# Fused recurrence, MoE and SwiGLU kernel: raw weight loads behind the capacity branch, and a rewritten attention tail

## The chip, the cores and the metric

The kernel runs on one core of one Trainium2 chip. The metric is device microseconds of one launch, inputs and outputs in device memory. Lower is better.

## The reference, cut to what matters

Three layers follow each other. A decayed recurrence over 768 steps (2 batches, 8 heads of width 48) gives 1536 rows of 384 values. A top-1 mixture of 8 experts with a capacity of 384 rows each maps them to 1536 rows, and a SwiGLU layer of inner width 1536 gives the output.

```python
cur = np.einsum('bhd,bhe->bhde', u[None] * kt, vt)
y[:, :, t] = np.einsum('bhd,bhde->bhe', rt, state + cur)
state = wt[:, :, :, None] * state + np.einsum('bhd,bhe->bhde', kt, vt)
...
expert_idx = np.argmax(x @ w_gate, axis=1)       # probs: softmax of the same logits
# rows go to their expert's slots in order, up to capacity
h = np.maximum(np.einsum('ecd,edf->ecf', disp, w1), 0.0)
y = np.einsum('ecf,efd->ecd', h, w2)
out[i] = gate_w[i] * y[expert_idx[i], pos[i]]    # rows that were kept
...
return (silu(x @ w_gate) * (x @ w_val) @ w_out)
```

## The kernel before

**Stages.** The sequence is cut into 12 units of 128 rows (u = 0 to 11, six per batch). A loop does units 0 to 9, and a hand-written piece of straight code, the tail, does the rest of units 10 and 11 and the routing of the last rows. Then comes a branch, then the expert stage (8 experts, at most 240 rows each), then SwiGLU. There is no scheduler: every engine gets its instructions in the order in which the Python code is written, and each waits on semaphores.

**Routing.** Rows are routed in four groups: units 0 to 3, 4 to 7 (`four`), 8 and 9 (`two`), 10 and 11 (`last`). For a group, `chosen_of` gives the steps that find the best expert from the gate products `lg` (`mx`, `eq`, `ls`, `be`, `ohs`, all on DVE, with one `ex` on ACT); `count` numbers the rows per expert on PE; `place` turns this into row addresses `slots`. `rows...` scale the rows into `xg` on ACT, and `scatter` writes them by address to the DRAM buffer `scr`, an indirect DMA on the POOL queue.

**Expert 0.** Its input is not read back whole. The rows of `two` and `last` that belong to it are picked by products with one-hot matrices `hot`: `x0_high` (ACT) and `x0_low` (DVE) split a scaled row block `xhl` into a high and a low half, `x0_add` (L810) adds its product to three PSUM tiles, and the rows scattered earlier come in through `zrow`, read back by `x0_load`. `parts` (L815, L816) then writes the operand `xe0`. The first product of expert 0 reads `xe0`.

**The branch.** `totals` and `offsets` give the counts `cnti`. Every engine loads one of them (L1096) and branches (L1223) around code for overfull experts (label `rare`), which is not taken here. The compiler counts DMA completions and instructions on semaphores, one for each of the eight hardware DMA queues and each engine. On the path that is not taken, each semaphore must be raised by what the skipped code would have added. The instruction for this waits first until everything issued earlier on that semaphore is done. SP does it for the eight DMA queues:

```text
SP L1223 EventSemaphore: wait DMAHW1 >= 144, then add 848
```

ACT's first instruction of expert 0, the ReLU at L1290, waits for all eight raised values, because its tile lies on memory that the skipped code also uses.

**Weights.** Raw float32 weights are loaded in pieces of 768 KB (`raw`, L169) by `load_raws`, as far as buffers are free: four and two from the start, three more (`more_raws(RAWS[2])`) in the tail once the attention buffers are closed by `early.close()`. A raw piece is cut into three parts; each is cast on ACT (`high`, L207) and its remainder computed on DVE (`low`, L212) into one of four, later seven, slots `wu`. These steps stand in a list, and `fill(us)` takes the next ones from it, as much as a credit in microseconds allows (a `low` costs 0.6, a `high` nothing); `need` forces them.

**Expert products.** `m1` (L1284) makes a [128, 240] tile from nine products into one of four PSUM buffers; `relu` (ACT L1290, DVE L1291) frees it; `m2` (L1302) follows after eight such tiles. `warm(n)` (L452) issues n products whose result nobody reads.

## Time and profile before

| | |
|---|---|
| median of 3 runs | 475.51 us (473.94, 475.51, 476.43) |
| profiled execution | 477.18 us, its span 475.5 us |
| PE busy | 452.9 us (95%), 3579 products |
| DVE busy | 332.6 us (70%) |
| ACT busy | 240.3 us (51%) |
| POOL busy | 69.3 us (15%) |
| share of PE in the chain that ended last | 72% |

The span runs from the first to the last instruction; the run's own time has 1.7 us around it. The loop over units lasts until about 78 us, the tail until about 100 us, the experts until about 243 us, and SwiGLU to the end. A product of PE is listed with a modelled end, so products that follow each other overlap in the listing. The granted clock of TensorE is given as a share of full speed, 1.00 or 0.50.

### The profile page before, as it was taken

What the parts mean: (1) busy time and instruction counts of PE and PEld (TensorE: products, weight loads), DVE (VectorE), ACT (ScalarE), POOL (GpSimd) and SP (SyncE); (2) the same over time, 40 slices, a digit from 0 to 9 for tenths busy, and PEclk for the clock granted to TensorE, in tenths of its full rate; (3) what the DMA queues carried; (4) which work ended last, traced back from release to release, by engine and by line L of the source; (5) the groups of instructions that cost most, each with busy time, mean ns of one, the idle gap of its engine ahead of it and who ended that gap; (6) DMA issues with size and microseconds to landing.
All of it is one profiled execution on the core that took longest, in us unless ns stands there. A gap on an engine that the chain in (4) does not pass through costs nothing.

```text
span 475.5 us, 9303 instructions
## 1 busy us (share of the span) xinstructions
PE 452.9 (95%) x3579; PEld 400.9 (84%) x3590; DVE 332.6 (70%) x705; ACT 240.3 (51%) x561; POOL 69.3 (15%) x87
## 2 busy tenths in 40 slices
PE   6998899777999999999999999999999999999994
PEld 3676677667999999999988888888888888888884
DVE  8999999836798658559779966575868576434241
ACT  4566775715788677665455465353525333221220
POOL 3323365430000000000000370000000000003033
PEclk9999999987999999999999999999999999999999
DMA  7899993393989965027323425042200000001011
GB/s 241 191 299 283 323 260 138 108 324 101 287 279 342 307 240 187 12 68 217 116 78 123 71 64 116 17 121 80 66 1 1 2 0 1 0 1 66 0 68 66
DMA packets 33649, 62.57 MB, mean 132 GB/s; under 512 B 5216, under 2 KB 16992, under 8 KB 33600
## 3 DMA queue, kind: packets, MB, share of 16 engines
q1 hardware_dynamic: 31680, 57.20, 40.0%
q0 software_dynamic: 1920, 4.73, 2.7%
q8 instruction: 29, 0.48, 0.4%
q14 instruction: 20, 0.16, 0.1%
HBM read 52.48 MB, written 9.44 MB: 130 GB/s over the span
## 4 chain that ended last, share of the span: by engine, by line
PE 72%; issue 2%; DVE 1%; POOL 1%; POOLq 0%; ACT 0%; ACTq 0%
PE psg L1395 31%; PE psu L1418 14%; PE pso L1302 14%; PE psh L1284 13%; POOL out L1430 1%; PE psx L1269 1%; DVE acc L1428 0%; DVE wu L212 0%; POOLq L1534 0%; DVE h L1291 0%; ACT h L1290 0%; POOLq L1430 0%; ACTq L1290 0%
## 5 line engine op out<-in xcount | busy, mean ns | idle before, releaser
L1395 PE MATMUL psg<-yb,wu 128*128 128x512 f32 x648 | 156.3, 395 | 0.0
L1395 PEld LDWEIGHTS psg<-yb,wu 128*128 128x128 f32 x648 | 121.3, 188 | 26.2
L1418 PE MATMUL psu<-wu,a 128*128 128x384 f32 x432 | 80.8, 336 | 0.0
L1418 PEld LDWEIGHTS psu<-wu,a 128*128 128x128 f32 x432 | 76.4, 188 | 2.9
L1284 PE MATMUL psh<-xe,wu 128*128 128x240 f32 x576 | 72.4, 283 | 6.2 <-DVE h L1291 4.4
L1284 PEld LDWEIGHTS psh<-xe,wu 128*128 128x128 f32 x576 | 68.8, 196 | 7.1 <-DVE h L1291 4.6
L1302 PE MATMUL pso<-h,wu 128*128 128x240 f32 x576 | 66.4, 275 | 0.0
L1302 PEld LDWEIGHTS pso<-h,wu 128*128 128x128 f32 x576 | 65.4, 189 | 0.0
L212 DVE TENSOR_TENSOR wu<-raw,wu 128x512 fp32r<-128x512 f32 x96 | 61.7, 683 | 0.0
L1402 DVE TENSOR_TENSOR t<-t,psg 128x512 f32<-128x512 f32 x36 | 24.7, 686 | 52.6 <-PE psg L1395 35.6
L207 ACT CAST wu<-raw 128x512 fp32r<-128x512 f32 x96 | 55.1, 621 | 3.4 <-PE pso L1302 1.4
L1407 ACT CAST a<-t 128x512 fp32r<-128x512 f32 x36 | 22.3, 619 | 58.2 <-DVE t L1402 58.2
L1291 DVE SCALAR_TENSOR_TENSOR h<-psh,h 128x240 fp32r<-128x240 f32 x64 | 24.9, 402 | 32.3 <-ACT h L1290 32.1
L1317 POOL DMA_INDIRECT idl<-ids,dests x12 | 13.4, 1120 | 171.5 <-DVE bits L187 168.2
L207 ACT CAST wu<-bits 128x384 fp32r<-128x384 f32 x36 | 18.0, 514 | 40.0 <-DVE bits L200 40.0
L1430 POOL DMA_INDIRECT out<-acc,idc x12 | 11.7, 976 | 174.1 <-DVE acc L1428 172.3
L1401 ACT ACTIVATE t<-psg 128x512 f32<-128x512 f32 x36 | 21.4, 595 | 27.5 <-PE psg L1395 27.5
L1290 ACT ACTIVATE h<-psh 128x240 fp32r<-128x240 f32 x64 | 23.3, 374 | 19.3 <-PE psh L1284 10.4
L1408 DVE TENSOR_TENSOR a<-t,a 128x512 fp32r<-128x512 f32 x36 | 24.8, 689 | 11.7 <-ACT a L1407 11.7
L1428 DVE TENSOR_TENSOR acc<-psu,acc 128x384 f32<-128x384 f32 x24 | 12.9, 558 | 20.8 <-PE psu L1418 20.8
L465 ACT COPY A<-psA 128x512 f32<-128x512 f32 x24 | 12.8, 587 | 18.8 <-PE psA L463 18.8
L466 POOL TENSOR_SCALAR_AFFINE_SELECT A<-A 128x512 f32<-128x512 f32 x24 | 15.2, 657 | 44.3 <-ACT A L465 44.3
(154 smaller groups left out, 558.1 us busy)
## 6 DMA issues: line engine op xcount, KB each, us to landing
raw<-in_moe_w SPq DMA_DIRECT2D x32, 768.0 KB, 6.7
dm<-in_dm SPq DMA_DIRECT2D x18, 291.0 KB, 6.7
scr<-zrow SPq DMA_DIRECT2D x12, 384.0 KB, 7.2
raw<-in_moe_w_gate SPq DMA_DIRECT2D x6, 768.0 KB, 4.3
raw<-in_moe_w_val SPq DMA_DIRECT2D x6, 768.0 KB, 4.4
raw<-in_moe_w_out SPq DMA_DIRECT2D x6, 768.0 KB, 4.3
v<-in_tk SPq DMA_DIRECT2D x12, 192.0 KB, 7.8
dm<-in_dm SPq DMA_DIRECT2D x3, 512.0 KB, 5.7
```

The lines of the kernel that those rows point to most:

```text
L207: nc.scalar.copy(out=slot_t[u % NSLOT][:, 0, c:c + n], in_=bits[i])
L212: nc.vector.tensor_tensor(out=w[:, 1, c:c + n], in0=bits.pop(i), in1=R(w[:, 0, c:c + n]), op=ALU.subtract)
L1284: nc.tensor.matmul(ps, w[:, a, k, c0:c0 + 128], xet[e][:, b, k, :], start=n == 0, stop=n == 8)
L1290: nc.scalar.activation(out=h[:, 0, :], in_=ps, func=AF.Relu)
L1291: nc.vector.scalar_tensor_tensor(out=h[:, 1, :], in0=ps, scalar=0.0, in1=R(h[:, 0, :]), op0=ALU.max, op1=ALU.subtract)
L1302: nc.tensor.matmul(ypt[e, d], w[:, a, f % 4, 128 * d:128 * d + 128], h[:, b, :], start=f == 0 and n == 0, stop=f == 7 and n == 2)
L1395: nc.tensor.matmul(gps[i][g], w[:, a, g, k, c0:c0 + 128], yb[t, k][:, c], start=a_ == k == 0, stop=a_ == k == 2)
L1401: nc.scalar.activation(out=t, in_=pg[0], func=AF.Silu)
L1402: nc.vector.tensor_tensor(out=t, in0=t, in1=pg[1], op=ALU.mult)
L1407: nc.scalar.copy(out=a[:, 0], in_=t)
L1408: nc.vector.tensor_tensor(out=a[:, 1], in0=t, in1=R(a[:, 0]), op=ALU.subtract)
L1418: nc.tensor.matmul(out_ps[t, j], att[i][:, c, 128 * j:128 * j + 128], w[:, a, f % 4, :], start=f % FP == 0 and n == 0, stop=f % FP == FP - ...
```

## The change

1. `load_raws` does nothing while `st["held"]` is set. It is set at the start of the tail and cleared behind the branch, after `x_load(1)`; six raw pieces are then issued at once. `early.close()` and `more_raws(RAWS[2])` move behind the tail and behind the branch.
2. The six casts of weight units 0 and 1, formerly three in the loop at u = 5 and three in the tail, stand in the loop at u = 6 and u = 8. The three `low` steps of unit 0 stay in the tail, at other places.
3. In the tail, `values(u + 1, [1, 2, 3])` is one run; `prep3` (DVE tile `rk`) comes after the placing of `four`; `count(two)` comes after `logits(u)`; the scatters of `four` follow their rows one by one; those of `two` move from ahead of the last products to behind them.
4. The low halves of `two` are made on GpSimd from `xg` (`xhl<-xg,xhl`), and their six products move behind those of the high halves of `last`.
5. `warm(2)` goes, and `warm(3)` comes after `count(last)`.

```diff
-            if i > 1:
+            wsteps += [(u, 0.6, low, j) for j in range(4) if i == 6]
...
+            if i > 5:
...
+        if q in xgs:
+            nc.gpsimd.tensor_tensor(out=lo, in0=xgs[q], in1=R(hi), op=ALU.subtract)
+            return
...
-        if u >= 5:
-            fill(0.0)
+        if u in (6, 8):
+            for _ in range(3):
+                step()
...
+    st["held"] = True
...
-    prep3(u + 1)
-    values(u, [2])
-    gate_t(u - 1)
     place(four)
...
     flush()
-    rows4[0]()
+    prep3(u + 1)
+    values(u, [2])
+    gate_t(u - 1)
...
-    values(u + 1, [1, 2])
+    values(u + 1, [1, 2, 3])
+    fill(0.6, 3.0)
...
-    early.close()
-    more_raws(RAWS[2])
-    load_raws(len(raws_))
...
-    x0_add(xhl[two[0]][0], hot[0][:, 0, :], 0, first=True)
-    for i, q in enumerate(two):
-        x0_low(q, sm2[:, i, :])
     for f in rows2:
         f()
+    for i, q in enumerate(two):
+        x0_low(q, sm2[:, i, :])
+    fill(0.6, 3.0)
     judge()
...
-        x0_add(xhl[q][1], hot[0][:, i, :], 0)
+        x0_add(xhl[q][0], hot[0][:, i, :], 0, first=not i)
...
     count(last)
+    warm(3, ps1, "T")
     atl, bases, placed, after = place(last)
-    for f in (*bases, *sums):
+    for f in (*bases, *placed, *sums):
         f()
+    tc.mark_branch_hint_location("rare", engines=[DVE, ACT, POOL])
+    for i, q in enumerate(last):
+        x0_high(q, sm[:, i, :])
+    for i in range(2):
+        onehot(2 + i, *(x[:, i, :] for x in atl))
     flush()
-    for f in later:
-        f()
+    later[0]()
+    totals(ps1, ones, (ohacc, *(ohs[:, q, :] for q in (*two, *last))), odds)
+    offsets(one8)
+    for i, q in enumerate(last):
+        x0_add(xhl[q][0], hot[0][:, 2 + i, :], 0)
+    for i, q in enumerate(two):
+        x0_add(xhl[q][1], hot[0][:, i, :], 0)
...
+    for f in later[1:]:
+        f()
     for q in two:
         scatter(q)
...
     x_load(1)
+    st["held"] = False
+    load_raws(len(raws_))
```

**SP at the branch.** Before, the last rows of SP ahead of the branch: the two reads of `zrow`, four raw pieces, then the load of the count.

```order
L784 DMA zrow<-scr 128x384
L784 DMA zrow<-scr 112x384
L169 DMA raw<-in_moe_w 128x4x384 x2
L169 DMA raw<-in_moe_w 128x3x512 x2
L1096 TENSOR_LOAD cnti
L1223 COMPARE_AND_BRANCH
```

Now, the same place of SP:

```order
L340 DMA v<-in_tk 128x384
L785 DMA zrow<-scr 128x384
L785 DMA zrow<-scr 112x384
L1100 TENSOR_LOAD cnti
L1227 COMPARE_AND_BRANCH
```

And now, SP behind the branch, where the reads of expert 1's rows (`xr`) come first:

```order
L1264 DMA xr<-scr 128x384
L1264 DMA xr<-scr 112x384
L169 DMA raw<-in_moe_w 128x4x384 x2
L169 DMA raw<-in_moe_w 128x3x512 x2
L169 DMA raw<-in_moe_w 128x4x384 x2
L1264 DMA xr<-scr 128x384
```

The four raw pieces went from ahead of the branch to behind it and behind `xr`; two more follow them there.

**DVE, the last choice.** Before, DVE between the best-expert steps of `last` and its one-hot matrices (`within` and `odds` judge the recurrence, `pcs` to `slots` finish the places of `two`):

```order
L580 RECIPROCAL sm<-sm 128x2
L386 TENSOR_SCALAR within<-within 128x1
L389 TENSOR_SCALAR odds<-within 128x1
L680 COPY pcs<-lg 128x16
L700 TENSOR_SCALAR end_1613<-sl 128x2
L703 TENSOR_TENSOR end<-end,sl 128x2
L706 TENSOR_TENSOR slots<-end,end_1613 128x2
L695 TENSOR_TENSOR t_1696<-lg,ohs 128x16
L670 TENSOR_REDUCE sl<-t_1696 128x2
L790 TENSOR_SCALAR hot<-col,end,sl 128x240 x2
```

Now:

```order
L696 TENSOR_TENSOR t_1682<-lg,ohs 128x16
L671 TENSOR_REDUCE sl<-t_1682 128x2
L624 TENSOR_REDUCE sm<-ex 128x2
L578 TENSOR_SCALAR sm<-sm 128x2
L581 RECIPROCAL sm<-sm 128x2
L791 TENSOR_SCALAR hot<-col,end,sl 128x240 x2
L387 TENSOR_SCALAR within<-within 128x1
L390 TENSOR_SCALAR odds<-within 128x1
L681 COPY pcs<-lg 128x16
```

Six small steps that stood ahead of `hot` stand behind it.

**DVE, unit 9 and 10.** Before, `rk`, which PE's gate products of unit 11 read, came straight after the row block `x` of unit 9, ahead of the placing of `four`:

```order
L527 TENSOR_TENSOR x<-y,aV 128x384
L428 TENSOR_TENSOR rk<-dm_112 128x512
L658 TENSOR_SCALAR t_1485<-lg 128x32
L661 TENSOR_TENSOR t_1486<-lg,csb 128x32
L680 COPY pcs<-lg 128x32
L664 TENSOR_TENSOR t_1486<-t_1486,t_1485 128x32
```

Now, the end of the same stretch:

```order
L581 RECIPROCAL sm<-sm 128x4
L671 TENSOR_REDUCE sl<-t_1475 128x4
L674 CAST slots<-sl 128x4
L678 TENSOR_REDUCE ohacc<-ohs 128x8
L429 TENSOR_TENSOR rk<-dm_112 128x512
L528 TENSOR_TENSOR x<-y,aV 128x384
```

`rk` went behind eleven small steps, to the place right ahead of the row block of unit 10.

## Rows read from the trace of the kernel before

**Rows 1.** The chain that ended last, in order of time, at expert 7
```profile
226.84 8.06 PE psh L1284 x72
```
**Rows 2.** Busy time by stretch: PE, PEld, DVE, ACT, POOL; granted clock; DMA share; GB/s
```profile
95.00:100.00 5.00, 4.46 (x24) 4.14 (x23) 3.51 (x15) 2.05 (x5) 3.57 (x4) 0.66 0.95 299
100.00:105.00 5.00, 4.30 (x36) 4.11 (x36) 0.30 (x1) 0.00 (x0) 0.69 (x1) 1.00 1.01 371
110.00:115.00 5.00, 4.35 (x19) 3.79 (x18) 3.58 (x8) 2.64 (x8) 0.00 (x0) 0.50 0.60 177
```
**Rows 3.** Timeline around the branch: start, duration, instruction, idle time and its releaser
```profile
100.61 4.30 PE L1284 MATMUL psh<-xe,wu 128*128 128x240 f32 x36 [1.15 <-ACTq L1223]
108.42 0.37 ACT L1290 ACTIVATE h<-psh 128x240 fp32r<-128x240 f32 x1 [8.56 <-SPq L1223]
...
109.28 1.21 PE L1284 MATMUL psh<-xe,wu 128*128 128x240 f32 x4 [4.37 <-DVE h L1291]
...
117.28 2.18 PE L1302 MATMUL pso<-h,wu 128*128 128x240 f32 x18
```
**Rows 4.** Line L1223, the branch: count, duration in ns, first and last start
```profile
L1223 SPq EVENT_SEMAPHORE  x9: 17/17/17, 97.8 to 108.3; - x9
...
L1223 ACTq EVENT_SEMAPHORE  x2: 17/17/17, 100.5 to 100.6; - x2
```
**Rows 5.** SP in the timeline, then DMA issues of 94 to 101 us (landing time last)
```profile
92.81 2.12 SPq L169 DMA_DIRECT2D raw<-in_moe_w  x4
...
raw<-in_moe_w SPq DMA_DIRECT2D x2, 768.0 KB, 13.9
```
**Rows 6.** The page's costliest groups, two of DVE: count | busy us, mean ns | idle
```profile
L212 DVE TENSOR_TENSOR wu<-raw,wu 128x512 fp32r<-128x512 f32 x96 | 61.7, 683 | 0.0
...
L1291 DVE SCALAR_TENSOR_TENSOR h<-psh,h 128x240 fp32r<-128x240 f32 x64 | 24.9, 402 | 32.3 <-ACT h L1290 32.1
```
**Rows 7.** Landing times: scatters of 84 to 92 us, of 94 to 108, raw pieces to 130
```profile
DMA to landing us min/median/max: 2.6/2.8/3.1
...
DMA to landing us min/median/max: 6.9/7.0/7.7
...
DMA to landing us min/median/max: 4.4/9.2/14.9
```
**Rows 8.** Timeline of ACT, two places in the loop and one at expert 0
```profile
67.55 1.07 ACT L465 COPY A<-psA 128x512 f32<-128x512 f32 x2 [2.06 <-PE psA L463]
...
73.09 0.38 ACT L400 COPY wm<-dm 128x224 f32<-128x224 f32 x1 [1.62 <-DMA dm<-in_dm]
...
122.48 3.22 ACT L207 CAST wu<-raw 128x512 fp32r<-128x512 f32 x6
```
**Rows 9.** Timeline of DVE in the tail
```profile
81.46 1.01 DVE L428 TENSOR_TENSOR rk<-dm 128x512 f32<-128x512 f32 x1
...
91.38 0.17 DVE L606 TENSOR_REDUCE mx<-lg 128x2 f32<-128x16 f32 x1 [0.41 <-PE lg L565]
...
93.20 0.13 DVE L386 TENSOR_SCALAR within<-within 128x1 f32<-128x1 f32 x1
...
94.26 0.72 DVE L790 TENSOR_SCALAR hot<-col,end,sl 128x240 fp32r<-128x240 f32 x2
...
95.05 1.14 DVE L804 SCALAR_TENSOR_TENSOR xhl<-x,sm,xhl 128x384 fp32r<-128x384 f32 x2
```
**Rows 10.** Timeline of PE in the tail
```profile
82.61 0.43 PE L435 MATMUL psr<-rk,ud 128*32 128x128 f32 x8
...
83.18 0.39 PE L488 MATMUL y<-Sb,M 128*64 128x96 f32 x4
...
94.81 2.11 PE L810 MATMUL x<-hot,xhl 128*128 128x240 f32 x10 [0.87 <-DVE hot L790]
```
**Rows 11.** Timeline: a GpSimd product and a small DVE step beside it
```profile
82.93 0.83 POOL L443 TENSOR_TENSOR aV<-v,a 128x384 f32<-128x384 f32 x1
...
83.04 0.77 DVE L667 TENSOR_TENSOR t<-t,ohs 128x32 f32<-128x32 f32 x1
```

More of the change, by code (lines that the diff above doesn't have):

```diff
@@ L128, in build @@
     raw_t, bits, mags, soon = {}, {}, {}, []
-    st = dict(loaded=0, step=0, freed=0, ahead=0.0, made=0)
+    st = dict(loaded=0, step=0, freed=0, ahead=0.0, made=0, held=False)
     def wu(key):
@@ L157, in load_raws @@
     def load_raws(upto):
-        while st["loaded"] < min(upto, len(raws_)):
+        while not st["held"] and st["loaded"] < min(upto, len(raws_)):
             free_ = [p for p in rps if len(p[2]) < p[1] or p[2][-p[1]] in done]
@@ L940, in build @@
     warm(1, ps1, "xT")
+    for f in c4:
+        f()
     scores(u + 1)
@@ L943, in build @@
     expand(u)
-    for f in c4:
-        f()
     values(u, [1])
@@ L948, in build @@
     xrow(u - 1)
-    prep3(u + 1)
-    values(u, [2])
-    gate_t(u - 1)
     place(four)
-    tick()
     for f in sums4:
@@ L957, in build @@
     flush()
-    rows4[0]()
+    prep3(u + 1)
+    values(u, [2])
+    gate_t(u - 1)
     psr = ps1.tile([128, C], F32, tag="xT", name="psr")
     gate_rows(u - 2, u + 1, psr)
+    rows4[0]()
+    scatter(four[0])
     gss[u - 1] = gp.tile([128, C], F32, tag="gs", name="gs", bufs=1)
@@ L963, in build @@
     rows4[1]()
+    scatter(four[1])
     values(u, [3])
@@ L968, in build @@
     xrow(u)
-    fill(1.2, 3.0)
+    own(u + 1, nc.vector)
     rows4[2]()
-    own(u + 1, nc.vector)
+    scatter(four[2])
     gate_t(u)
-    values(u + 1, [1, 2])
+    values(u + 1, [1, 2, 3])
+    fill(0.6, 3.0)
     c2, sums2, rows2, sm2 = chosen_of(two)
@@ L977, in build @@
     rows4[3]()
-    for q in (*ready, *four):
-        scatter(q)
+    scatter(four[3])
     x0_load()
-    early.close()
-    more_raws(RAWS[2])
-    load_raws(len(raws_))
+    xrow(u + 1)
+    logits(u)
+    count(two)
     for f in sums2:
         f()
-    count(two)
+    gate_t(u + 1)
     at2, bases, placed, later = place(two)
@@ L989, in build @@
         f()
-    values(u + 1, [3])
     for i, q in enumerate(two):
         x0_high(q, sm2[:, i, :])
-    xrow(u + 1)
-    logits(u)
-    warm(2)
     for i in range(2):
         onehot(i, *(x[:, i, :] for x in at2))
-    gate_t(u + 1)
-    x0_add(xhl[two[0]][0], hot[0][:, 0, :], 0, first=True)
+    for f in rows2:
+        f()
     for i, q in enumerate(two):
         x0_low(q, sm2[:, i, :])
-    for f in rows2:
-        f()
+    fill(0.6, 3.0)
     judge()
@@ L1006, in build @@
     logits(u + 1)
-    x0_add(xhl[two[1]][0], hot[0][:, 1, :], 0)
     for i, q in enumerate(two):
-        x0_add(xhl[q][1], hot[0][:, i, :], 0)
+        x0_add(xhl[q][0], hot[0][:, i, :], 0, first=not i)
     c, sums, rows, sm = chosen_of(last)
@@ L1013, in build @@
     count(last)
+    warm(3, ps1, "T")
     atl, bases, placed, after = place(last)
-    for f in (*bases, *sums):
+    for f in (*bases, *placed, *sums):
         f()
-    flush()
-    for f in later:
+    tc.mark_branch_hint_location("rare", engines=[DVE, ACT, POOL])
[3 more added lines that the diff above has]
+        onehot(2 + i, *(x[:, i, :] for x in atl))
+    flush()
+    later[0]()
[5 more added lines that the diff above has]
+        x0_add(xhl[q][1], hot[0][:, i, :], 0)
+    for i, q in enumerate(last):
+        x0_low(q, sm[:, i, :])
+    x0_add(xhl[last[0]][1], hot[0][:, 2, :], 0)
+    for f in later[1:]:
         f()
@@ L1021, in build @@
         scatter(q)
-    tc.mark_branch_hint_location("rare", engines=[DVE, ACT, POOL])
-    for i, q in enumerate(last):
-        x0_high(q, sm[:, i, :])
-    for f in placed:
-        f()
-    for i in range(2):
-        onehot(2 + i, *(x[:, i, :] for x in atl))
-    totals(ps1, ones, (ohacc, *(ohs[:, q, :] for q in (*two, *last))), odds)
-    for i, q in enumerate(last):
-        x0_add(xhl[q][0], hot[0][:, 2 + i, :], 0)
-    for i, q in enumerate(last):
-        x0_low(q, sm[:, i, :])
-    x0_add(xhl[last[0]][1], hot[0][:, 2, :], 0)
-    offsets(one8)
     fill(0.6, 3.0)
@@ L1050, in build @@
         parts(x0ps[k], k, xe0)
+    early.close()
     at.close()
@@ L1236, in build @@
                     overflow(e, s0, min(C, capb - s0), *pools)
+    more_raws(RAWS[2])
     NB, TB = 3, 512
```

## The prediction

> **What bounds the kernel now.** I read the page first, for the share of PE in the chain of work that ended last (72%), and then that chain in order of time. From expert 0's second half on it is PE without a gap: expert 7's 72 first-layer products take 8.06 us [rows 1], 0.112 us each, and what comes later only shifts with them. A gain must come from ahead, where PE waits. The busy time by stretch shows two poor places: the granted clock is 0.66 of full speed from 95 to 100 us, and 0.50 from 110 to 115 us [rows 2], the lower level, 1.2 GHz, after PE had stood. The timeline gives the place in between: PE starts expert 0 at 100.61, fills its four PSUM buffers in 4.30 us, then stands 4.37 us until DVE has freed one; DVE waited for ACT, and ACT 8.56 us for SP's line L1223 [rows 3]. The view of that line names the cause: ACT itself was through the branch at 100.6, while SP's nine semaphore raises run from 97.8 to 108.3 [rows 4]. Each waits for all that was issued before on its DMA queue, and the last things issued there were four raw weight pieces from 92.81 on; the two pieces issued from 94 us on took a median of 13.9 us to land, which puts them near 108 [rows 5]. So expert 0 waits for weights that it does not read.
>
> **The change part by part.**
>
> *Raw loads behind the branch.* With no raw piece in flight, SP's queues hold only the two zrow reads, issued before 92.81 and read by PE before the branch anyway. SP's raises can then end at about 99, as its first one came at 97.8, and ACT's ReLU waits only for the first nine products. PE no longer stands: 4.37 us. The rest of the first layer, 36 products from 109.28 to the second layer's first product at 117.28, took 8.00 us [rows 3], at half clock [rows 2]; by expert 7's rate they take half of 8.06, 4.03, so 3.97 us more. Sum -8.3 us. What is late next there is DVE: per tile a ReLU half and a weight remainder, 0.40 + 0.68 us on average [rows 6], against 1.01 us for PE's nine products. Its list of steps behind the branch is the same as before. The remainder of the third weight part has to be there for the fifth tile's second half; I take 0.2 us of stall (0 to 0.9, one step late by one tile).
>
> *Do the raw pieces come too late?* SP now issues the xr reads first, which wait for the last scatter, then six pieces. Scatters took a median of 7.0 us to land beside raw traffic and 2.8 us without [rows 7]. With the last one issued near 103 (my estimate: four of them, each over 1 us, behind DVE's last lows near 99), xr goes at about 106 and the first piece lands near 112, taking 4.4 us, the shortest row, after one queued xr [rows 7]. Its casts stand in the run of six from 122.48 (two of unit 5, three of unit 6, one more) [rows 8], shifted by 7 us to about 116.5; the second piece follows at about 114.5 against 118. So this costs 0, on 3 us of slack; ACT's ReLUs are queued behind these casts, and PE behind the ReLUs.
>
> *rk behind the placing of four.* DVE does the same work up to the row block x of unit 10, but before it had rk done at 82.5, ahead of eleven small steps [rows 9]. Now rk comes last, and PE's gate products and the last values of unit 10 come behind it: from 82.61 to 83.18 and 0.39 more [rows 10], about 1.0 us. DVE waits meanwhile, and its later steps follow. The two low halves taken from DVE (1.14 us a pair, [rows 9]) make room, but one weight remainder of 0.68 us now stands there too, and DVE's idle time ahead of mx was 0.41 us [rows 9]. Step by step I get mx of the last group at 92.4 instead of 91.38: +1.0 us (0 to 1.1).
>
> *Six small steps behind hot.* From the first of them at 93.20 to hot at 94.26 are 1.06 us [rows 9], of which two dependent steps of 0.2 us each stay ahead of hot: -0.65 us.
>
> *Low halves on GpSimd.* They run beside DVE's last choice. A GpSimd product of this size took 0.83 us, and a small DVE step beside it 0.77 us [rows 11], where 0.17 is usual for a small one [rows 9]: some 0.6 us lost in one product. For two products the bounds are 0 and 1.66 us (DVE shut out for both); I take 0.5, the one row at hand. The Trainium skill, page "SBUF — State Buffer", section "Who interferes with whom", says that a DVE instruction with two SBUF inputs and a GpSimd instruction that reads SBUF exclude each other, the later one blocking until the other ends; the row agrees, as that step ended when the GpSimd product did. By the rule alone the term would be up to 1.66 us, the upper bound that I had already.
>
> *The last products.* Behind hot PE now has 18 one-hot products instead of 12, beside the same zrow ones, but cps, the counts and the low halves of last on DVE pace them, as hot is followed by eight small steps every 0.2 us, with cps among them, and the lows (1.14 us, [rows 9]). With the last third of the products behind them at full clock I get their end 4.1 us after that of hot. Before it was 4.5 us: hot ends at 94.98 [rows 9], and PE was idle for 1.15 us before 100.61 [rows 3]; there they ran at 0.21 us each, ten in 2.11 us [rows 10], partly on the low clock. If the clock falls again the six added products and the rest cost 1.0 us more than before. Three idle products fill some of PE's pause ahead of them; the trace of before can't show whether that is enough. I take +0.3 (-0.4 to +1.0).
>
> *Casts in the loop.* Six cost 3.22 us [rows 8], so three about 1.6. Behind unit 8 they fit into ACT's wait for a DMA (1.62 us idle before 73.09); behind unit 6 they delay copies that have 2.06 us to catch up before 67.55 [rows 8]. DVE sets the loop's pace: +0.1 (0 to 1.6 if the cover at unit 6 fails).
>
> Moving the scatters of two behind the products lets POOL end some 3 us later; only xr waits for that, with its slack above. Buffers closed later cost nothing, as no other load waits for that memory.
>
> Sum: -8.3 + 0.2 + 1.0 - 0.65 + 0.5 + 0.3 + 0.1 = -6.85 us. The profiled run took 477.18 us with a span of 475.5; its like would be 470.3. Against the median of the three runs, 475.51, the forecast is **468.7 us**.
>
> **The rivals.** (a) *The tail gives back more.* GpSimd's products shut DVE out for both (+1.2 over my value) and the clock stays low in the last products (+0.7), with a late third remainder (+0.7): 468.7 + 2.6 = 471.3. For it: the blocked step [rows 11], and the low clock at this very place [rows 2]. Against it: most of DVE's steps there are too short to meet both products. (b) *The tail gets shorter.* rk costs nothing (-1.0), no contention (-0.5), full clock (-0.7): 466.5. For it: PE has fewer pauses in the tail. Against it: the order shows PE behind rk. (c) *The wait is not the raw loads'.* If ACT's 8.56 us had another cause, such as fetching the code behind the branch, the change keeps only the tail's +1.25: 476.8, within measuring error of no change. Against it: the raises are spread over 10 us, and ACT's own pair came at 100.5 [rows 4]. (d) *Slower: the held weights starve expert 1.* The casts block ACT in order, so that PE runs dry at about 123, when its four buffers are full. The second piece, issued near 107, decides: it must land after 123 to cost anything, that is 16 us, above the longest landing of 14.9 us [rows 7]; at twice that longest, near 137, it costs 14 us: 468.7 + 14 = 483.
>
> **How the numbers follow.** Forecast 0.62, (a) 0.18, (b) 0.10, (c) 0.06, (d) 0.04. About 0.5% is what a measurement of this kernel can tell from no change, 2.4 us here; forecast, (a) and (b) all lie beyond it on the faster side. That gives faster 0.90, same 0.06 from (c), slower 0.04 from (d). The range takes the bounds of the terms: all low, -8.3 + 0 + 0 - 0.65 + 0 - 0.4 + 0 = -9.35, 466.2; the upper end takes (a) with 1 us of loop or stall on top, 472.3.
>
> **What the profile will show.** Right: SP's raises at L1223 end before 100; ACT's first ReLU starts about 1.2 us after the first product of expert 0; that product starts between 100 and 102.5; PE shows no pause over 1 us and a clock of 1.00 from there; the second layer starts about 8.3 us behind it, near 110. The raw casts of unit 6 wait less than 1 us for their DMA. Wrong: if the raises still last beyond 104, or if the first product comes after 103 (then the tail's terms are too small), or if ACT stands for a raw piece between 114 and 123 while PE's buffers fill.

## The result, and the profile after

The changed kernel takes 479.03 us (median of 19 runs, 477.49 to 485.82) against 476.43 us for the kernel before (19 runs). The ratio is 1.0062 with a 95% interval of 1.0035 to 1.0088: slower by about 0.6%, a little more than a measurement can tell from no change. The forecast was 468.7 us with a range of 466.2 to 472.3. The profiled run took 481.57 us, its span 479.9 us, 4.4 us more than the span of before.

**The branch went as forecast.** The view of the branch's line (L1227 now; columns: queue and instruction, count, shortest/median/longest in ns, first and last start) shows SP's nine raises within 0.6 us, where they took 10.5 us before [rows 4]:

```profile
L1227 SPq EVENT_SEMAPHORE  x9: 17/17/17, 104.5 to 105.1; - x9
L1227 ACTq EVENT_SEMAPHORE  x2: 17/17/17, 109.0 to 109.0; - x2
```

The timeline of the changed kernel behind the branch (columns: start, duration, engine and line, then what ended the idle time ahead of it) shows all 72 products of expert 0's first layer in one row of 8.54 us and the first ReLU 1.44 us behind their start:

```profile
109.02 8.54 PE L1289 MATMUL psh<-xe,wu 128*128 128x240 f32 x72 [1.33 <-ACTq L1227]
...
110.46 0.37 ACT L1295 ACTIVATE h<-psh 128x240 fp32r<-128x240 f32 x1 [2.38 <-PE psh L1289]
...
117.39 2.18 PE L1307 MATMUL pso<-h,wu 128*128 128x240 f32 x18
```

From the first product to the second layer are 8.37 us, where there were 16.67 [rows 3]. But the first product comes at 109.02 instead of 100.61, so the second layer starts at 117.39, against 117.28 before. The tail has given back all of the gain.

**In the tail, PE stands once and then runs at half clock.** The busy time by stretch (columns: stretch, its length, busy us of PE, PE's weight loads, DVE, ACT and POOL with instruction counts, granted clock, DMA share, GB/s) of the changed kernel:

```profile
80.00:85.00 5.00, 3.66 (x66) 2.82 (x62) 4.25 (x21) 2.62 (x7) 2.03 (x3) 1.00 0.02 5
85.00:90.00 5.00, 4.15 (x45) 3.71 (x46) 1.26 (x3) 1.02 (x3) 2.00 (x2) 0.54 0.19 73
90.00:95.00 5.00, 5.00 (x53) 4.58 (x54) 3.18 (x14) 1.87 (x5) 2.21 (x2) 0.50 0.18 64
...
100.00:105.00 5.00, 4.18 (x29) 3.36 (x30) 4.28 (x23) 2.13 (x4) 0.00 (x0) 0.50 0.00 0
```

The clock falls to 0.50 between 85 and 90 us and stays there to beyond 105, although PE is busy for all of 90 to 95. Before, it fell between 95 and 100 [rows 2]. The timeline of the changed kernel shows PE's pause just ahead of the fall, and the last choice further on:

```profile
83.73 0.78 DVE L668 TENSOR_TENSOR t<-t,ohs 128x32 f32<-128x32 f32 x1
...
85.02 0.68 DVE L429 TENSOR_TENSOR rk<-dm 128x512 f32<-128x512 f32 x1
85.70 1.03 POOL L736 DMA_INDIRECT scr<-xg,slots  x1 [1.24 <-DVE rk L429]
...
85.85 0.66 PE L436 MATMUL psr<-rk,ud 128*32 128x128 f32 x8 [2.08 <-DVE rk L429]
...
97.97 1.95 POOL L806 TENSOR_TENSOR xhl<-xg,xhl 128x384 fp32r<-128x384 f32 x2 [3.74 <-ACT xg L586]
...
98.32 0.68 DVE L615 TENSOR_TENSOR eq<-eq,csb 128x16 f32<-128x16 f32 x1
...
99.24 0.71 DVE L621 TENSOR_TENSOR ohs<-eq,be 128x16 bf16<-128x16 f32 x1
```

rk ends at 85.70 and PE has stood 2.08 us for it; before, rk started at 81.46 [rows 9] and the gate products ran at 82.61 [rows 10]. Two small DVE steps beside GpSimd's pair take 0.68 and 0.71 us instead of 0.17.

**And a wait that was not there before.** In expert 1's first layer PE stands for the rows of expert 2:

```profile
112.01 0.80 SPq L1264 DMA_DIRECT2D xr<-scr  x2
...
112.85 7.04 SPq L169 DMA_DIRECT2D raw<-in_moe_w  x6
...
120.00 3.05 SPq L1264 DMA_DIRECT2D xr<-scr  x2
...
126.12 3.19 PE L1289 MATMUL psh<-xe,wu 128*128 128x240 f32 x27
...
131.78 0.52 PE L1274 MATMUL psx<-ident,xr 128*128 128x128 f32 x3 [2.48 <-DMA xr<-scr]
```

SP issues the six raw pieces for 7 us and the two xr reads of expert 2 only then; the longest landing of an xr read in this stretch is 11.6 us, where it was 5.1 before. The stretch from 130 to 135 us has a granted clock of 0.82. What follows the second layer's start takes 362.5 us (479.9 - 117.39) against 358.2 (475.5 - 117.28): 4.3 us more.

So the 4.4 us are: the tail starts 1.0 us later (first idle product of the tail at 80.12 against 79.11; a_xr_casts below shows why), it takes 7.4 us longer up to the first product, the branch gives 8.3 back, and xr costs 4.3.

### The profile page after: what moved, and what is told of

It is laid out like the page before. It is cut to its first block, busy times and chain, and to the rows that moved or that the text cites. A ratio compares the mean times of both kernels' runs of the same rounds, so it can differ in the third digit from the quotient of the medians.

```text
span 479.9 us, 9303 instructions
## 1 busy us (share of the span) xinstructions
PE 457.4 (95%) x3580; PEld 404.9 (84%) x3591; DVE 334.5 (70%) x703; ACT 240.3 (50%) x561; POOL 70.9 (15%) x89
## 4 chain that ended last, share of the span: by engine, by line
PE 70%; DMA 2%; issue 2%; POOL 1%; DVE 0%; POOLq 0%; SPq 0%; ACT 0%; ACTq 0%
PE psg L1402 31%; PE psu L1425 14%; PE psh L1289 13%; PE pso L1307 12%; DMA xr<-scr 2%; POOL out L1437 1%; PE psx L1274 1%; DVE acc L1435 0%; SPq L169 0%; POOLq L1541 0%; ACT wu L207 0%; POOLq L1437 0%; ACTq L207 0%; ACT h L1295 0%; SPq L1264 0%
## 5 line engine op out<-in xcount | busy, mean ns | idle before, releaser
L1289 PE MATMUL psh<-xe,wu 128*128 128x240 f32 x576 | 70.7, 281 | 1.3 <-ACTq L1227 1.3
L1289 PEld LDWEIGHTS psh<-xe,wu 128*128 128x128 f32 x576 | 67.8, 194 | 1.6 <-ACTq L1227 1.5
L1295 ACT ACTIVATE h<-psh 128x240 fp32r<-128x240 f32 x64 | 23.2, 372 | 11.3 <-PE psh L1289 10.5
L1319 DVE TENSOR_TENSOR yb<-yT,yb 128x512 fp32r<-128x512 f32 x27 | 18.5, 686 | 4.4 <-ACT yb L1318 4.4
```

What stands on the lines that cost most here:

```text
L1289: nc.tensor.matmul(ps, w[:, a, k, c0:c0 + 128], xet[e][:, b, k, :], start=n == 0, stop=n == 8)
L1295: nc.scalar.activation(out=h[:, 0, :], in_=ps, func=AF.Relu)
```

## The experiments

Each set of kernels ran on one chip, with the kernel before beside it (its medians in the four sets are 477.0 to 477.4 us); the sets ran on different chips, so where kernels of two sets are compared, the profiles have to carry it. Two measures read from each profile make the kernels comparable, whenever the loop ended: the **tail**, from its first idle product to expert 0's first product, and the **first layer**, from there to the second layer's first product. "Clock" is the granted clock over the tail.

| kernel | median us | ratio to before, 95% | tail us | clock | first layer us |
|---|---|---|---|---|---|
| before | 476.43 | 1 | 21.50 | 0.92 | 16.67 |
| changed | 479.03 | 1.0035 to 1.0088 | 28.90 | 0.65 | 8.37 |
| h_hold | 473.52 | 0.9908 to 0.9982 | 24.76 | 0.72 | 9.81 |
| h_hold_xr | 472.53 | 0.9886 to 0.9951 | 24.75 | 0.72 | 11.20 |
| a_xr | 477.04 | 0.9972 to 1.0032 | 28.41 | 0.70 | 8.39 |
| a_rk | 478.79 | 1.0016 to 1.0077 | 27.04 | 0.75 | 8.37 |
| a_xr_warm | 473.87 | 0.9912 to 0.9963 | 25.06 | 0.80 | 8.37 |
| a_xr_casts | 476.87 | 0.9971 to 1.0028 | 28.83 | 0.64 | 8.56 |
| a_xr_dve | 479.13 | 1.0003 to 1.0065 | 29.26 | 0.65 | 8.60 |
| h_xr_warm | 468.59 | 0.9783 to 0.9873 | 20.18 | 1.00 | 8.49 |
| b_warm | 478.02 | 0.9992 to 1.0050 | 20.19 | 1.00 | 17.66 |
| h_warm | 471.33 | 0.9820 to 0.9900 | 20.19 | 1.00 | 8.51 |
| a_xr_warm2 | 473.84 | 0.9883 to 0.9953 | 23.33 | 1.00 | 8.38 |
| a_rk_xr_warm2 | 470.83 | 0.9824 to 0.9899 | 21.34 | 1.00 | 8.38 |
| f_dve | 475.71 | 0.9955 to 1.0007 | 25.47 | 0.80 | 9.64 |
| f_casts | 473.94 | 0.9901 to 0.9963 | 24.03 | 0.86 | 9.06 |
| after_warm | 478.32 | 1.0005 to 1.0064 | 23.39 | 1.00 | 8.96 |
| best_again | 471.58 | 0.9864 to 0.9933 | 22.13 | 0.92 | 8.37 |

**First set: the parts of the change alone.** h_hold puts the hold into the kernel before.

```diff
-        while st["loaded"] < min(upto, len(raws_)):
+        while not st["held"] and st["loaded"] < min(upto, len(raws_)):
...
     four, two, last = (ended[q] for q in (7, 9, 11))
+    st["held"] = True
...
-    early.close()
-    more_raws(RAWS[2])
-    load_raws(len(raws_))
...
+    more_raws(RAWS[2])
     NB, TB = 3, 512
...
     x_load(1)
+    st["held"] = False
+    load_raws(len(raws_))
```

> The kernel before with one part alone: raw weights held from the tail until behind the branch, tail and loop as before. Theory (the branch gain stands by itself; the changed tail gave back 8.4 us and xr of expert 2, queued behind six raw pieces, another 4.3): the first product of expert 0 stays near 100.6, the second layer starts 8.3 us earlier, near 109.0, and PE then waits for xr of expert 2 in expert 1's first layer, 2 to 4.3 us with the low clock behind it. So 4.0 to 6.3 us faster than before. Rival (holding the pieces itself makes the branch come late, or starves the casts): the first product after 104, or PE waiting for weights, and no gain or a loss.

Measured: 3.6 us under the median of before in its set (477.14), and no wait for xr. The first product comes at 104.47, neither at 100.6 nor with a wait for weights; the second layer starts at 114.28, 3.0 us earlier than before:

```profile
104.47 9.97 PE L1284 MATMUL psh<-xe,wu 128*128 128x240 f32 x72 [1.15 <-ACTq L1222]
...
114.28 2.18 PE L1302 MATMUL pso<-h,wu 128*128 128x240 f32 x18
```

The stretches show why: the old tail, with no instruction changed but the loads, also fell to the lower clock, earlier than in the profile of before, and stayed there into the first layer. It fell inside a pause of 1.43 us that is taken up at the end.

```profile
85.00:90.00 5.00, 4.08 (x58) 3.31 (x58) 3.92 (x17) 4.84 (x12) 3.46 (x4) 1.00 0.23 82
90.00:95.00 5.00, 3.66 (x16) 3.27 (x16) 2.74 (x9) 1.70 (x6) 0.79 (x1) 0.55 0.42 152
```

So the tail's clock is a loss that both tails can have. The theory was right on the sign and wrong on what gives the gain back.

h_hold_xr also takes xr of expert 2 ahead of the raw pieces:

```diff
     x_load(1)
+    x_load(2)
     st["held"] = False
...
         relu(e, 7)
-        x_load(e + 2)
+        if e:
+            x_load(e + 2)
```

> The same, with the two xr reads of expert 2 issued ahead of the six raw pieces instead of behind them. Theory (xr of expert 2 is late because it stands behind the raw pieces): PE has no wait for xr, the clock stays at 1.00 from the first product on, 7.8 to 8.5 us faster than before. Rival (the wait there comes from the late raw pieces, or from scatters that land late, not from the place in the queue): within 1 us of the kernel with the hold alone.

Measured: 1.0 us under h_hold, as its rival said, with overlapping intervals; the clock was low here as well, so this run could not tell.

a_xr is that edit in the changed kernel.

> The changed kernel with the two xr reads of expert 2 ahead of the six raw pieces. Theory: the 2.5 us wait of PE for xr at 131.78 and the low clock behind it go, 4.0 to 4.5 us less than the changed kernel, that is 1.0 to 2.0 us under the kernel before. Rival (the late tail delays the scatters, and so the xr reads, whatever their place): less than 1.5 us gained on the changed kernel.

Measured: 2.0 us under the changed kernel (2.7 when each is set against the kernel before of its own measurement), no difference from before: less than the theory's 4.0 and more than the rival's 1.5. In the profile the wait is gone, and from the second layer on it takes 358.2 us (span 476.7, second layer at 118.49), the same as before: the 4.3 us of that stretch are xr's place in the queue. The medians show only part of it; the profiled run of the changed kernel was 2.5 us above its own median.

a_rk puts rk back in the changed kernel:

```diff
+    prep3(u + 1)
+    values(u, [2])
+    gate_t(u - 1)
     place(four)
...
     flush()
-    prep3(u + 1)
-    values(u, [2])
-    gate_t(u - 1)
```

> The changed kernel with rk, the third values of unit 10 and the transposes for the gate put back ahead of the placing of four, as in the kernel before. Theory (rk behind the placing leaves PE idle for 2.08 us at 83.8, the clock falls to the lower level and the rest of the tail runs on it): gate products near 83.8 instead of 85.85, granted clock 1.00 from 85 to 95, first product of expert 0 at 103 to 104.5 instead of 109.0, 4.5 to 6 us less than the changed kernel. Rival (the clock falls because of the later pauses, or the loss is in the loop's casts and GpSimd's products): under 2.2 us gained, and the clock still 0.5 from 90 to 100.

Measured: the gate products come 3.49 us behind the first idle product, as before, instead of 5.73, so rk's place costs 2.2 us on PE. But the median gains only 0.2 us: the clock held to 93.4 (granted 0.84 from 90 to 95 us, 0.50 behind) and fell then, inside another pause. DVE's row block x of unit 11 waited 3.31 us, and PE for it:

```profile
93.81 0.56 DVE L528 TENSOR_TENSOR x<-y,aV 128x384 f32<-128x384 f32 x1 [3.31 <-remote]
```

This pause is taken up at the end. Removing one pause was not enough to hold the clock.

**Second set: idle products against the clock.** a_xr_warm adds eight to a_xr where PE waits for rk:

```diff
+    warm(8)
     gate_rows(u - 2, u + 1, psr)
```

> The changed kernel with xr of expert 2 ahead of the raw pieces and eight idle products of 512 columns ahead of the gate products, where PE stands 2.1 us for rk. Theory (PE's pause there makes the clock fall, and the tail then runs at half clock): granted clock 1.00 from 85 to at least 94, first product of expert 0 three to four us earlier than in the kernel with xr first alone (110.1 in its profile), and 2 to 4 us less in the median, 473 to 475. Rival (the later pauses make the clock fall anyway, or the idle products only take PE's time): within 1 us of it.

Measured: 473.87 us, 3.2 under a_xr and 3.0 under a_xr_casts of its own set, as the theory expected. The gate products now wait 0.26 us and run at the same distance behind the first idle product (5.64 us), so the products cost PE nothing. The clock holds at 1.00 to 90 and is 0.79 from 90 to 95; the theory had it hold to 94:

```profile
85.84 0.42 PE L436 MATMUL psr<-rk,ud 128*32 128x128 f32 x8 [0.26 <-DVE rk L429]
```

h_xr_warm has hold and xr first in the old tail, and ten idle products in three pauses of it:

```diff
     for f in sums2:
         f()
+    warm(3)
     count(two)
...
     count(last)
+    warm(4, ps1, "T")
...
     totals(ps1, ones, (ohacc, *(ohs[:, q, :] for q in (*two, *last))), odds)
+    warm(3, ps1, "T")
```

> The kernel before with the raw weights held, xr of expert 2 ahead of them, and idle products in three pauses of the old tail: three ahead of the counts of two, four behind the counts of last, three behind the totals. Theory (of the 8.3 us only 4.3 show with the hold because the tail's clock falls at 90.5 and stays low until the first layer): the clock stays 1.00 to the first product of expert 0, which comes at 100.5 to 101.5, 3 to 4 us less than the kernel with hold and xr first (472.5), so 468 to 469.5. Rival (the fall is not due to PE's pauses, or the idle products stand in PE's way): within 1 us of 472.5 or slower.

Measured: 468.59 us, 3.9 under h_hold_xr and 1.7% under before. The clock is 1.00 in every stretch of the tail, and the first layer takes 8.49 us instead of 16.67, which is the branch term whole. (The second layer starts at 109.13, 8.15 us earlier than before, as a tail that is 1.32 us shorter starts 1.35 us later.)

```profile
90.00:95.00 5.00, 4.81 (x41) 3.55 (x41) 4.31 (x22) 3.02 (x9) 1.23 (x2) 1.00 0.37 124
95.00:100.00 5.00, 4.30 (x34) 3.23 (x32) 4.61 (x22) 3.38 (x8) 2.53 (x3) 1.00 0.22 78
```

One caution: h_hold_xr ran on another chip, and its profile has the pause taken up at the end, which this one has not. So what the idle products do for the old tail's clock is not separated here from that pause.

a_xr_casts takes the loop's casts back in a_xr:

```diff
-        if u in (6, 8):
-            for _ in range(3):
-                step()
+        if u >= 5:
+            fill(0.0)
```

The list of the steps is also as before, a remainder following its cast two places later from the third cast on.

> The changed kernel with xr of expert 2 ahead of the raw pieces and the loop's casts of weights as before (from unit 5 on whatever is free of cost, instead of three each in units 6 and 8). Theory: the loop's copies start 1.1 us earlier, so 0.8 to 1.5 us less than the kernel with xr first alone (477.0). Rival (ACT only moves its waiting, as forecast): within 0.4 us of it.

Measured: 0.2 us in the median, nothing that can be told. The profiles do tell. The tail starts at 78.99 to 80.46 in the nine with the old form of the loop and at 80.12 to 82.07 in the nine with the new one; in every set each kernel with the old form but h_xr_warm starts ahead of all with the new. The loop shows where: from DVE's row block x of unit 6 to that of unit 7 are 7.28 to 7.30 us in all nine profiles with the new form, and 6.45 to 6.48 in eight of the nine with the old (6.00 in h_xr_warm, whose earlier block came late); here it is 6.47. In the changed kernel, these rows lie between the two blocks:

```profile
60.66 1.66 ACT L207 CAST wu<-raw 128x512 fp32r<-128x512 f32 x3
...
62.79 1.05 ACT L466 COPY A<-psA 128x512 f32<-128x512 f32 x2
...
64.60 1.05 DVE L416 TENSOR_TENSOR M<-dm,X 128x512 f32<-128x512 f32 x1
...
65.08 1.26 POOL L444 TENSOR_TENSOR aV<-v,a 128x384 f32<-128x384 f32 x1
...
65.57 1.31 DVE L419 TENSOR_TENSOR M<-dm,R 128x512 f32<-128x512 f32 x1
...
68.63 0.52 DVE L528 TENSOR_TENSOR x<-y,aV 128x384 f32<-128x384 f32 x1
```

And in the kernel before:

```profile
61.36 1.06 ACT L465 COPY A<-psA 128x512 f32<-128x512 f32 x2
...
63.26 1.20 POOL L443 TENSOR_TENSOR aV<-v,a 128x384 f32<-128x384 f32 x1
...
64.93 0.66 DVE L415 TENSOR_TENSOR M<-dm,X 128x512 f32<-128x512 f32 x1
...
65.51 0.68 DVE L418 TENSOR_TENSOR M<-dm,R 128x512 f32<-128x512 f32 x1
...
67.93 0.53 DVE L527 TENSOR_TENSOR x<-y,aV 128x384 f32<-128x384 f32 x1
```

The three casts put ACT's copies of A back by 1.4 us, GpSimd works on A behind them and starts aV 1.8 us later, and two of DVE's steps that had come behind aV now run beside it and the step on A ahead of it, and take 1.02 us more together. (The two scans R ahead of them take 0.2 less, 1.70 us instead of 1.91.) ACT does catch up, as forecast; DVE does not.

a_xr_dve takes the two low halves from GpSimd to DVE:

```diff
-            nc.gpsimd.tensor_tensor(out=lo, in0=xgs[q], in1=R(hi), op=ALU.subtract)
+            nc.vector.tensor_tensor(out=lo, in0=xgs[q], in1=R(hi), op=ALU.subtract)
```

> The changed kernel with xr of expert 2 ahead of the raw pieces and the first two low halves on DVE instead of GpSimd, at the same place in the order. Theory (GpSimd's pair shuts DVE out of two steps of the last choice, 1.05 us, while DVE's own pair would cost 1.2 us): within 0.5 us of the kernel with xr first alone. Rival (the contention is a main part of the tail's loss): 1 us or more faster.

Measured: 2.1 us slower than a_xr, which ran on another chip, and the intervals overlap. Neither case was met; it brought no gain, and that DVE's own pair costs more than the steps that GpSimd blocks is not shown.

**Third set: the terms at full clock.** b_warm is the kernel before with the ten idle products of h_xr_warm and nothing else.

> The kernel before with the ten idle products in the three pauses of its tail, and nothing else: raw weights loaded in the tail as before. Theory (the first ReLU is held to 108.4 by the raw pieces in flight, however early the tail ends): at most 1.5 us faster than before, with PE's 4 us pause behind the first 36 products still there. Rival (the idle products by themselves make most of the 8 us by which hold, xr first and idle products beat the kernel before): 4 us or more faster.

Measured: no difference from before. The tail is as short as h_xr_warm's, 20.19 us, and PE then stands even longer for the raw pieces in flight:

```profile
99.68 4.47 PE L1287 MATMUL psh<-xe,wu 128*128 128x240 f32 x36 [1.15 <-ACTq L1226]
...
109.72 1.21 PE L1287 MATMUL psh<-xe,wu 128*128 128x240 f32 x4 [5.56 <-DVE h L1294]
```

So neither part does it alone: without the hold, a shorter tail gains nothing.

h_warm is h_xr_warm without xr first.

> The kernel before with the raw weights held and the ten idle products, xr of expert 2 behind the raw pieces as in the changed kernel. Theory (with the old tail the last scatter lands early, xr goes in time, and its place costs nothing): within 1 us of 468.6. Rival (xr behind six pieces costs PE a wait here too): 2 us or more slower than 468.6, with a wait for xr in expert 1's first layer.

Measured: 2.7 us slower than h_xr_warm, with the wait of the rival, from the view of the waits (total us, count, longest):

```profile
PE psx L1272 <- DMA xr<-scr: 3.0, 1, 3.0
```

The theory missed here: from the second layer on it takes 362.7 us, so xr's place costs as much with the old tail, once the tail is fast. In h_hold PE came to that point 10.6 us after the reads were issued (115.45 to 126.02) and they had landed; here it came after 9.6 us, and the longest landing was 12.5.

b_warm and h_warm ran on one chip and differ by the hold alone: 17.66 against 8.51 us of first layer. This is the cleanest sight of the branch term.

a_xr_warm2 has more idle products in the changed tail:

```diff
+    warm(8)
     gate_rows(u - 2, u + 1, psr)
...
+    warm(2, ps1, "xT")
     gate_t(u + 1)
...
+    warm(2, ps1, "xT")
     logits(u + 1)
...
-    warm(3, ps1, "T")
+    warm(6, ps1, "T")
```

> The changed kernel with xr first, eight idle products ahead of the gate products, two ahead of each of the last two groups of transposes and gate columns, and six instead of three behind the counts of last. Theory (what is left of the changed tail's loss once the clock holds is rk's 2.2 us): clock 1.00 up to the first product of expert 0, which comes at 101.5 to 103, and 470 to 471.5. Rival (the clock falls all the same, as at 92.9 with the eight alone): 473 to 474.5.

Measured: the clock held, the tail took 23.33 us, but the median, 473.84, is the rival's. The first product came at 104.41, since this tail started at 81.08, and at full clock the changed tail is 3.15 us longer than the old one, not 2.2. The choice of the last group begins 13.35 us behind the tail's start, where h_xr_warm has it at 12.25 (92.71 - 80.46):

```profile
94.43 0.17 DVE L607 TENSOR_REDUCE mx<-lg 128x2 f32<-128x16 f32 x1
```

A 1.7 us wait for xr of expert 3 stands in this profile too.

a_rk_xr_warm2 is the same with rk back and without the eight.

> The changed kernel with rk back ahead of the placing of four, xr first, and the idle products of the kernel beside it but for the eight ahead of the gate products, where PE no longer waits. Theory (rk's place costs 2.2 us on PE's path, and putting it back alone brought nothing because the clock fell further on): 1.5 to 2.5 us less than the kernel beside it, 468 to 469.5. Rival (rk's place costs nothing at full clock, or the clock falls without the eight): the same as the kernel beside it, or slower.

Measured: 3.0 us under a_xr_warm2, the tail 1.99 us shorter. rk's place costs 2 us at full clock. What is left is 1.16 us against the old tail. The timeline of this kernel shows it: three blocked or waiting steps where the old tail has none.

```profile
91.66 0.16 DVE L607 TENSOR_REDUCE mx<-lg 128x2 f32<-128x16 f32 x1
...
92.16 1.94 POOL L806 TENSOR_TENSOR xhl<-xg,xhl 128x384 fp32r<-128x384 f32 x2 [0.80 <-ACT xg L586]
...
92.48 0.69 DVE L621 TENSOR_TENSOR ohs<-eq,be 128x16 bf16<-128x16 f32 x1
...
93.21 0.92 DVE L690 TENSOR_TENSOR t<-ohs,csb 128x16 f32<-128x16 bf16 x1
...
95.01 0.70 DVE L791 TENSOR_SCALAR hot<-col,end,sl 128x240 fp32r<-128x240 f32 x2
...
96.09 0.17 PE L756 MATMUL cps<-ohacc,ones 128*128 128x8 bf16 x1 [1.19 <-DVE pcs L681]
...
101.64 1.05 PE L1291 MATMUL psh<-xe,wu 128*128 128x240 f32 x7 [1.40 <-ACTq L1229]
```

The same places in h_xr_warm's timeline:

```profile
92.71 0.18 DVE L606 TENSOR_REDUCE mx<-lg 128x2 f32<-128x16 f32 x1 [0.41 <-PE lg L565]
...
93.55 0.18 DVE L620 TENSOR_TENSOR ohs<-eq,be 128x16 bf16<-128x16 f32 x1
93.76 0.17 DVE L689 TENSOR_TENSOR t<-ohs,csb 128x16 f32<-128x16 bf16 x1
...
95.59 0.72 DVE L790 TENSOR_SCALAR hot<-col,end,sl 128x240 fp32r<-128x240 f32 x2
...
100.64 2.07 PE L1287 MATMUL psh<-xe,wu 128*128 128x240 f32 x15 [1.15 <-ACTq L1225]
```

From mx to hot are 3.35 us against 2.88, and from hot to the first product 6.63 against 5.05. Up to mx this tail is the shorter one, 11.36 us from its start against 12.25.

**Fourth set.** f_dve and f_casts are a_rk_xr_warm2 with the edits of a_xr_dve and of a_xr_casts.

> The changed kernel with rk back, xr first and idle products (470.8), and the low halves of two on DVE instead of GpSimd. Theory (GpSimd's pair blocks DVE in the choice of last for 1.3 us at full clock, while DVE's own pair there costs some 1.2 us on the same path): within 0.7 us of 470.8. Rival (GpSimd's pair is what the changed tail loses against the old one): 1.3 us or more faster.

> The changed kernel with rk back, xr first and idle products (470.8), and the loop's casts of weights as before. Theory (three casts in units 6 and 8 fit into ACT's waits): within 0.5 us of 470.8. Rival (they hold up the loop, as the later end of the loop in some profiles suggests): 1 us or more faster.

Measured: 475.71 and 473.94. On this chip the clock fell in both tails (0.80 and 0.86), and the pause of a_rk is there again (2.52 and 2.43 us), so they can't be set against 470.8 from another chip. The yardstick of this set (best_again, below) is 3.0 us above its first measurement; with that shift the medians show no cost of the casts, and again no gain from DVE. Both are weak. The loop of f_casts is again the shorter one: 6.46 us between the two row blocks against 7.30 in f_dve, and the tail starts at 79.24 against 80.15.

after_warm is the changed kernel with the idle products of a_xr_warm2 alone.

> The changed kernel with nothing but idle products: eight ahead of the gate products, two ahead of each of the last two groups of transposes and gate columns, six instead of three behind the counts of last; xr of expert 2 behind the raw pieces. Theory (clock and xr are separate losses): 2.5 to 4.5 us slower than the same with xr first (473.8), with a wait for xr of 2 to 3 us. Rival (at full clock the last scatter lands in time and the place of xr costs nothing): within 1 us of 473.8.

Measured: 4.5 us slower than a_xr_warm2, which ran on another chip, and a 3.9 us wait for xr, the longest of all. With the shorter tail PE stands ready for the transposes 4.4 us sooner than in the changed kernel (124.90 against 129.30), and SP issues the xr reads only 3.0 us sooner (116.99 against 120.00): clock and xr are separate losses, and the idle products alone are no cure.

best_again is h_xr_warm once more, unchanged.

> The kernel before with hold, xr first and ten idle products once more, beside the others on one chip: 468 to 469.5 expected if it is to be called faster than both kernels.

Measured: 471.58 us, outside what was expected, but 1.0% under before with an interval of 0.9864 to 0.9933. In its profile the clock was at the lower level between 93 and 96 us in spite of the idle products, and the pause was there too. The version beats the kernel before on both chips. That the clock makes the difference between 1.0 and 1.7% is not shown: the spans of the two profiles are only 0.9 us apart (468.5 and 467.6).

## Why the prediction was wrong, point by point

**The branch term was right.** -8.3 us and 0.2 of stall were forecast, and 16.67 - 8.37 = 8.30 was measured in the profile, 16.67 - 8.49 = 8.18 in h_xr_warm. Rival (c), that the raw loads are not what SP waits for, fell. Two of the announced signs failed for a reason outside this term: SP's raises end at 105.1, not before 100, and the first product comes after 103, the sign given for tail terms that are too small.

**rk's term came out, by a working that was in part luck.** +1.0 was forecast (0 to 1.1) as the shift of mx of the last group, and at full clock mx comes 13.35 us behind the tail's start instead of 12.25: +1.1. But the step priced only the PE products that now come behind rk and took DVE's order as neutral, and rk's place by itself costs 2.0 to 2.2. Its old place was cover: it ran while DVE waited for PE's counts of four. In the new place it starts behind all of DVE's placing steps (from 82.80, when the counts were there, to 85.02), among them the product that GpSimd's aV blocks for 0.78 us, a row that the prediction had in hand [rows 11] for another term. The other edits ahead of mx give 0.9 back (11.36 against 12.25 in a_rk_xr_warm2). The prediction names one of them, the two low halves taken from DVE; which of them it is was not tested.

**The clock's term was the large miss.** The prediction let the clock cost 1.0 us at most, in the last products, and asked only whether it falls "again" there. It put PE behind rk and did not ask what the pause that this opens, 2.08 us, does to the clock of all that follows. At full clock the changed tail takes 23.33 us, with its own clock 28.90: 5.57 us, against 21.50 - 20.18 = 1.32 us in the kernel before; net 4.25 us. That filling PE's pauses with idle work holds the clock is shown for the changed tail: on one chip a_xr_warm has 0.80 where a_xr_casts and a_xr_dve have 0.64 and 0.65, and with more idle products a_xr_warm2 and after_warm have 1.00. For the old tail the two kernels with the hold and without idle products ran on another chip and had the pause taken up at the end; best_again, with that pause and idle products, was low for 3.4 us (92.9 to 96.4), h_hold, with it and without them, for 17.1 (90.5 to 107.5). The Trainium skill, page "TensorE: Matmul & The Clock Gate", Part 1, calls the throttled clock the default state that activity releases. The runs with idle products agree with that; the changed kernel's rows add that the clock fell inside a pause of 2.08 us and stayed at the lower level for some 20 us, although PE is listed as busy for all of 90 to 95.

**Raw pieces: 0 forecast, and the weights did come in time, but xr did not.** The step followed the two pieces and their casts, and put SP's order down only up to the first of them. The xr reads of expert 2, written behind expert 0's first layer, stand on the same queue behind all six pieces. The order of SP shown with the change ends with just this read. Announced were no pause of PE over 1 us and a clock of 1.00 behind the first product; the reads' wait is 2.48 us, with a granted clock of 0.82 from 130 to 135. The view of SP was read for whom it makes wait at the branch, not for what is queued behind the moved loads. Rival (d) had the place; its size (14 us, where 4.3 were measured) and its victim (weights, where it was xr) were wrong, and its chance of 0.04 was too little.

**GpSimd's pair was mis-sized: +0.5 forecast of 0 to 1.66; measured 1.26** (0.69 + 0.92 against 0.18 + 0.17) at full clock, 1.05 in the changed kernel's profile. One row of another product was taken for the pair; the prediction held most of DVE's steps there too short to meet both products, and two of them met one each. The Trainium skill, page "SBUF — State Buffer", section "Who interferes with whom", says that a DVE instruction with two SBUF inputs contends with a GpSimd instruction that reads SBUF, and that one with at most one SBUF input, outside the 2-port modes, does not. The rows agree: eq, ohs and t, which read two SBUF tiles, were long, and mx and the sums between them, with one SBUF input or a PSUM one, kept 0.17. Doing the pair on DVE was no better in either trial.

**Six small steps: -0.65 forecast.** mx to hot grew by 0.47 with 1.26 of blocking in it, so the rest fell by 0.79: near the forecast.

**The last products were mis-sized: +0.3 forecast (-0.4 to +1.0), measured +1.58** at full clock. PE, in order, stands 1.19 us for the counts cps, which wait for pcs behind hot, and the six added products follow.

**Loop casts were mis-sized: +0.1 forecast, +1.0 measured** at the tail's start in the changed kernel's profile, inside the bound of 1.6 given for the case that the cover at unit 6 fails. The step looked for ACT's slack, and ACT does make up its time by 68.15; but GpSimd follows ACT's copies, and its late products collide with steps of DVE, which sets the loop's pace. As with GpSimd's pair, DVE's steps are long beside GpSimd's, here in a place where it was not looked for.

**DVE's stall behind the branch:** +0.2 forecast; the first layer's 8.37 us are 0.3 above expert 7's 8.06.

Added up for the profiled run: the tail's order +2.0 above the forecast (3.15 for 1.15: last products 1.3, GpSimd's pair and the small steps 0.6, mx 0.1), the clock +4.25, xr +4.3, the loop's casts +0.9, and the branch with its stall -0.2: 11.25 us, the distance between -6.85 and +4.4. The clock's net is an estimate from four profiles (changed, a_xr_warm2, before, h_xr_warm).

**The range** was too narrow because its ends were bounds of the listed terms. Two mechanisms, the clock behind a new pause and the reads behind the moved loads, were not on the list, and both work through what is next on the same engine or queue.

## What to carry to other kernels

Before an order is changed to fill one engine, look for pauses of TensorE that it opens: in these profiles a pause of 2 us cost more through the clock behind it than by itself, and idle products, which wait for nothing, took much or all of that loss away (a tail of 25.06 and 23.33 us instead of 28 to 29), at no cost where they fitted the pause. When loads are moved, write down what is queued behind their new place on the same queue, and move small reads with a deadline ahead of them. When work is put into an engine's slack, follow what its later output starts on other engines, and what that will run beside: ACT had the time for the casts, and the loop still lost 0.8 us at once. A gain that is real in its own stage (8.3 us here) shows in the total only if the stages around it keep their time: the hold alone gave 3.6, the idle products alone 0, and hold, idle products and the early xr reads together 5.5 to 8.8.

## What the runs showed of the hardware that was not expected

In six profiles DVE's row block x of unit 11 started 1.4 to 3.3 us late (h_hold 1.43, h_hold_xr 1.41, best_again 1.37, f_casts 2.43, f_dve 2.52, a_rk 3.31). Its only wait is for the last products of the values, whose modelled end lay that far ahead, and PE issued later products in the meantime. It was seen in two of the four sets alone, there in every kernel with rk in its old place and in none with rk behind the placing. Each time the clock fell during it or within 3 us behind it. Why the wait ended so late was not found, and it stays open. It stands where a_rk's gain went missing; that it is the reason was not tested.

One kernel with the same code, h_xr_warm and best_again, took 468.59 and 471.58 us on two chips, with the runs of each within 3.6 us. Their profiles differ by the granted clock in the tail, 1.00 and 0.92, by that pause and by the tail's start (80.46 and 78.99), and their spans by 0.9 us; what makes up the rest of the 3.0 us between the medians is not shown.
